# Moving ScalarE's guard work and the turning of K and B inside the steps of a fused recurrence and feed-forward kernel

## The chip, the cores and the metric

The kernel runs on one core of a Trainium2 chip. The metric is the device time of one execution in microseconds (us), the median of the runs shown. A core has five engines that run in parallel, each working off its own instructions in order: TensorE (PE in the profile; PEld is its loading of weights), VectorE (DVE), ScalarE (ACT), GpSimd (POOL) and SyncE (SP), which here only issues DMAs. TensorE writes its results to PSUM, a small memory of eight banks per partition; an engine that reads a PSUM buffer out sets when that buffer can be written again.

## The reference

Inputs r, k, v, w, a, b have the shape (4 batches, 8 heads, 768 tokens, 40). For each batch and head a 40x40 state is carried over the tokens, and its output goes through a feed-forward layer with squared ReLU:

```python
for t in range(S):
    y[:, :, t] = np.einsum('bhd,bhde->bhe', rt, state)
    Sa = np.einsum('bhde,bhe->bhd', state, at)
    state_decay = state * wt[:, :, None, :] - np.einsum('bhd,bhe->bhde', Sa, bt)
    state = state_decay + np.einsum('bhd,bhe->bhde', vt, kt)
...
x = attn_out.transpose(0, 2, 1, 3).reshape(B * S, H * D)
h = np.maximum(x @ w_in, 0.0)
out = (h * h) @ w_out        # w_in is 320 x 2048, w_out is 2048 x 320
```

## The kernel before

The 768 tokens are cut into 6 chunks of 128, so that the recurrence becomes matrix products inside a chunk and one hand-over from chunk to chunk. A chunk's 32 batch-head pairs are worked off in 8 steps of four heads: 48 steps `st` in all. Two steps make one batch m of inputs (one chunk of one batch, all eight heads, 24 of them). A loop over `st` (L603 on) writes the instructions of every engine in the order in which they are to run; nothing reorders them later. So a call's place in the loop's body is its place in the queue of each engine that it uses.

The names that matter:

- `st_a_mm` (ca on PE) and `st_a_ev` (CN on DVE, two instructions of 128x512): the masked products of the next step.
- `st_p`, `st_m`, `st_corr`, `st_c1`, `st_sn`: the inverse inside a chunk as a series. P is a PSUM tile; ScalarE copies it to Mc, PE adds a correction with Mc ("corr1", L339), DVE takes the difference c, PE adds a correction with c ("corr2", L339 again), and ScalarE copies the negated result, Sn, into the tile EVX (L355). POOL then makes x and Cc, where Cc waits for Sn.
- `st_jk` (L364): a square of the matrix N (a part of CN) with a running sum, on ScalarE; `st_energy` (L374, tile jm): squares of Mc or Cc of four earlier steps with a running sum, on ScalarE, in odd steps only. Both feed a guard that is tested after the loop (`ep`, L667). Each is two instructions: the activation and a short read of its accumulator.
- `st_t` (tb on PE, TB on DVE): Sn and the state U are transposed into one PSUM tile tb, Sn first, and copied to TB. `st_ex_mm` of the next step needs TB.
- `st_ex_mm`, `st_ex_ev`, `st_z`, `st_kb`, `st_y`: the output and the state (ex and uy on PE; EVX, YS and UZ on DVE).
- `filler(st)` takes the next piece of the feed-forward work of an earlier chunk; each step has three. In odd steps of the steady part the first two pieces are the two halves of an output (op, 8 matmuls each) and the third is a part of the hidden layer (hp, 6 matmuls); in even steps all three are hp. The copy that ends a piece runs on ScalarE: hs (ReLU) for hp, and osb, followed by the output DMA on SP, for the second half of op. With `hold=True` that copy is not written at once, but by `release()`, which comes behind `st_sn`; without it, it is written at once. The square of hs, Gt, runs on POOL, but for every fourth piece on DVE, and that one is put off to `flush()`, behind `st_t`. In the steady part it is the piece of the odd steps.
- `prepare(st, lot)` calls the steps by which a batch is prepared. For batches from 5 on: A's cast (POOL), the logarithm lnW (ACT), cs (PE), its two exponentials and KBp = K and B by an exponential (`prep_decay`: ACT, then POOL, odd steps), GA turned and copied (`prep_ga_mm`, `prep_ga_ev`: tt on PE, GT on ACT), AT (DVE), K and B turned and copied (`prep_kb`: 8 transposes into tt, then KBT on ACT, 128x1024), and the casts of V and R and two copies of V into EVX (POOL). The last ones, `prep_kb` and `prep_cast_rv`, have the lot 4, behind `st_t` and `flush()`.

hp, op, cs and tt share one PSUM tag, "ff", of two buffers, which they take in turn: each piece waits until the last piece but one has been copied out. P and tb share another, "sp".

Of the kernel before, what the change touches and what calls it, by code (L numbers as in the profile page):

```python
# [18 lines left out]
def kernel(  # L19
# [23 lines left out]
    NB, NHH, T, D = r.shape  # L43
# [4 lines left out]
    NQ = NP // 2  # L48
    NS = NCH * NQ
# [110 lines left out]
    def half(s):  # L160
        return slice(64 * s, 64 * s + 64)
# [132 lines left out]
    def st_a_mm(st):  # L294
        c, o, j0, p2, EVX = where(st)
        ca = CNs[st, "ps"] = [ps.tile([128, 2, 2, L], FP32, name=f"ca{s}", tag=f"ca{s}")
                              for s in range(2)]
        for u in range(2):
            for i in range(2):
                for s in range(2):  # L300
                    nc.tensor.matmul(out=ca[s][:, i, u, :], lhsT=o.KBT[half(s), u, j0 + i, :],  # L301
                                     rhs=o.AT[half(s), j0 + i, :], start=(i == 0 and u == 0),
                                     stop=True, skip_group_check=True)
# [7 lines left out]
    def st_p(st):  # L311
        c, o, j0, p2, EVX = where(st)
        CN, UZ = CNs[st], UZs[c % 2]
        P = Ps[st] = ps.tile([128, 2, 2, 64], FP32, name="P", tag="sp")
        if c > 0:
            for i in range(2):
                nc.tensor.matmul(
                    out=P[:, i, :, 0:D], lhsT=o.AT[:, j0 + i, :],
                    rhs=UZ[:, p2.start + i, :].rearrange("p (s d) -> p s d", s=2)[:, :, 0:D],
                    start=(i == 0), stop=False, skip_group_check=True)  # L320
        for i in range(2):
            for s in range(2):
                nc.tensor.matmul(out=P[:, i, s, 0:D], lhsT=CN[:, i, s, 0, :],  # L323
                                 rhs=EVX[:, i, s, L:LV], start=(c == 0 and i == 0 and s == 0),
                                 stop=False, skip_group_check=True)
# [18 lines left out]
    def st_c1(st):  # L344
        c, q = divmod(st, NQ)
        c1 = c1s[st] = qdp.tile([128, 4, D], BF16, name="c1", tag="c1")
        nc.vector.tensor_tensor(out=c1[:],  # L347
                                in0=Ps[st][:].rearrange("p i s e -> p (i s) e")[:, :, 0:D],
                                in1=Mc[c][:, q], op=ALU.subtract)
# [12 lines left out]
    def st_jk(st, CN):  # L362
        jk = qdp.tile([128, 2, 2, L], BF16, name="jk", tag="jk", bufs=1)
        nc.scalar.activation(out=jk[:], in_=CN[:, :, :, 1, :], func=ACTF.Square,  # L364
                             accum_out=ACC[:, AN + st:AN + st + 1])

    def st_energy(su):
        if su < 0 or su % 2 == 0:
            return
        hc = su // (NQ // 2)  # L370
        c, q = divmod(hc * (NQ // 2), NQ)
        src, at = ((Mc, AM), (Cc, AC))[su % (NQ // 2) // 2]
        jm = qdp.tile([128, NQ // 2, 4, D], BF16, name="jm", tag="jm", bufs=1)
        nc.scalar.activation(out=jm[:], in_=src[c][:, q:q + NQ // 2], func=ACTF.Square,  # L374
                             accum_out=ACC[:, at + hc:at + hc + 1])

    def st_t(st, su):
        tb = ps.tile([128, 4, 128], BF16, name="tb", tag="sp")
        if st < NS:
            EVX = EVXs[st % NEV]  # L380
            for i in range(2):
                for s in range(2):
                    nc.tensor.transpose(out=tb[half(s), i, :], in_=EVX[:, i, s, L + LV:EV],  # L383
                                        identity=IDb[:])
        if 0 <= su < NS - NQ:
            c, q = divmod(su, NQ)
            for i in range(2):
                for s in range(2):
                    nc.tensor.transpose(out=tb[half(s), 2 + i, :], identity=IDb[:],  # L389
                                        in_=UZs[(c + 1) % 2][:, 2 * q + i, half(s)])  # L390
        lo, hi = 0 if st < NS else 2, 4 if 0 <= su < NS - NQ else 2
        if lo < hi:
            TB = qdp.tile([128, 4, 128], BF16, name="TB", tag="TB", bufs=NQ + 2)
            nc.vector.tensor_copy(out=TB[:, lo:hi], in_=tb[:, lo:hi])  # L394
            SnTs[st] = TBs[su] = TB
# [3 lines left out]
    def st_ex_mm(st):  # L399
        c, o, j0, p2, EVX = where(st)  # L400
        SnT = SnTs.pop(st)
        ex = exs[st] = [ps.tile([128, 2, 2, L], FP32, name=f"ex{s}", tag=f"ex{s}")
                        for s in range(2)]
        for u in range(2):
            for i in range(2):
                for s in range(2):
                    lhsT = SnT[half(s), i, :] if u else o.RVT[half(s), 1, j0 + i, 0:L]
                    nc.tensor.matmul(out=ex[s][:, i, u, :], lhsT=lhsT,  # L408
                                     rhs=o.RVT[half(s), 0, j0 + i, 0:L],
                                     start=(i == 0 and u == 0), stop=True, skip_group_check=True)  # L410

    def st_ex_ev(st, s):
        EVX = EVXs[st % NEV]
        nc.vector.tensor_tensor(  # L414
            out=EVX[:, :, s, 0:2 * LV].rearrange("p i (u x) -> p i u x", u=2)[:, :, :, 0:L],
            in0=exs[st][s][:], in1=MEX[:].rearrange("p (i u) x -> p i u x", u=2), op=ALU.mult)
# [133 lines left out]
    def filler(st, hold=False):  # L550
        if fill and fill[0][0] <= st:
            fill.pop(0)[1](hold)
# [14 lines left out]
    for m in range(1, NBC):  # L567
        if m == 1:
            plan = ((-2, 1, prep_kb), (-2, 1, prep_ga), (-1, 4, prep_rv))
        elif m <= AHEAD:  # L570
            plan = ((-4, 5, prep_ln), (-4, 5, prep_decay), (-4, 5, prep_cast), (-3, 4, prep_kb),
                    (-3, 4, prep_ga), (-2, 4, prep_rv))
        else:
            plan = ((-4, "P" if m > AHEAD + 2 else 5, prep_new), (-4, 5, prep_ln),
                    (-3, "P", prep_decay), (-3, "C", prep_ga_mm), (-3, "C", prep_ga_ev),
                    (-3, "A", prep_at), (-3, 4, prep_kb), (-3, 4, prep_cast_rv),
                    (-2, "P", prep_v))
            plan += ((-2, 5, prep_turn),) if m >= 2 * NB else ((-1, 1, prep_rv),)
        if m >= AHEAD:
            plan += ((-9 if m == AHEAD else -7, 5, load),)  # L580
        for ds_, lot, f in plan:
            when.setdefault((2 * m + ds_, lot), []).append((f, m))

    def prepare(st, lot):
        for f, m in when.pop((st, lot), []):
            f(m)
# [15 lines left out]
    Ns = {}  # L602
    for st in range(NS + 2):  # L603
        late = st == 1
        if st + 1 < NS and not late:
            st_a_mm(st + 1)
        if 1 <= st <= NS:
            st_ex_mm(st - 1)
        if st < NS:
            st_p(st)  # L610
            st_m(st)
        if 1 <= st <= NS:
            st_jk(st - 1, Ns.pop(st - 1))
        if st >= 2:
            st_y(st - 2)
        if 1 <= st <= NS:
            st_ex_ev(st - 1, 0)
        prepare(st, "P")
        filler(st)
        if 1 <= st <= NS:  # L620
            st_z(st - 1)
        if st < NS:
            st_corr(st, Mc[st // NQ][:, st % NQ], False)
            st_c1(st)
        prepare(st, "C")
        if 1 <= st <= NS:
            st_ex_ev(st - 1, 1)
        prepare(st, "A")
        if st + 1 < NS and not late:
            st_a_ev(st + 1)  # L630
        filler(st, True)
        if st == 0:
            warm(8)
        prepare(st, 1)
        if st < NS:
            st_corr(st, c1s[st], True)
            Ns[st] = st_sn(st)
        release()
        if late:
            st_a_mm(st + 1)  # L640
        filler(st)
        st_t(st, st - 2)
        if late:
            st_a_ev(st + 1)
        flush()
        prepare(st, 4)
        if st >= NS - 4:
            filler(st)
        st_energy(st - NQ // 2)
        if 1 <= st <= NS:  # L650
            st_kb(st - 1)
        if 1 <= st <= NG:
            load_win(st - 1)
        if st == 4:
            load_wout()
        if st >= 2 and (st - 2) % (NQ // 2) == NQ // 2 - 1:
            h = (st - 2) // (NQ // 2)
            gather(*divmod(h, 2), [nc.sync] if st < NS + 1 else [nc.sync, nc.gpsimd, nc.sync])
            feed(st + 2, h)
        prepare(st, 5)  # L660
# [137 lines left out]
```

## Time and profile before

| what | us |
|---|---|
| runs shown: 311.32, 308.99, 312.38; median | 311.32 |
| the profiled execution's own time | 310.16 |
| its span, from the first to the last instruction | 308.4 |

Parts 1 and 2 of the profile's page: busy time of each engine, its share of the span and its instructions, and the span in 40 slices, where a digit is the busy share in tenths.

```profile
PE 281.4 (91%) x3746; PEld 212.1 (69%) x3746; DVE 221.1 (72%) x503; ACT 203.6 (66%) x529; POOL 210.2 (68%) x390
...
PE   7766887799999999999999999999999999898892
...
DVE  7456676798879878887978798788879776841140
ACT  3454336487688778777877887787787776645260
POOL 8575745388876887797779779777977886625200
PEclk9985755799999999999999999999999999979799
```

The first quarter, up to about 75 us, is the start: inputs and weights are loaded, and TensorE's granted clock is at half for a part of it. From about 78 to 260 us the steps run steadily. Behind it comes a tail, in which the rest of the feed-forward work drains.

Part 4, the chain of work that ended last, by engine, and two groups of part 5 (line, engine, operation, out<-in, count, busy time and mean of one in ns, idle time of the engine before them and what ended it):

```profile
PE 64%; ACT 21%; DVE 5%; issue 4%; POOL 3%; DVEq 0%; ACTq 0%; POOLq 0%
...
L364 ACT ACTIVATE jk<-CN 128x512 bf16<-128x512 bf16 x48 | 30.0, 624 | 0.0
```
```profile
L374 ACT ACTIVATE jm<-Mc 128x640 bf16<-128x640 bf16 x12 | 8.7, 728 | 0.0
L374 ACT ACTIVATE jm<-Cc 128x640 bf16<-128x640 bf16 x12 | 8.7, 728 | 0.0
```

A chain's shares say which engine's work each moment of the span is put down to, followed back from the last instruction. Durations of neighbours on one engine overlap by about 0.1 us, so sums of them are a little more than the time that they take.

### The profile page before, as it was taken

What the parts mean: (1) busy time and instruction counts of PE and PEld (TensorE: products, weight loads), DVE (VectorE), ACT (ScalarE), POOL (GpSimd) and SP (SyncE); (2) the same over time, 40 slices, a digit from 0 to 9 for tenths busy, and PEclk for the clock granted to TensorE, in tenths of its full rate; (3) what the DMA queues carried; (4) which work ended last, traced back from release to release, by engine and by line L of the source; (5) the groups of instructions that cost most, each with busy time, mean ns of one, the idle gap of its engine ahead of it and who ended that gap; (6) DMA issues with size and microseconds to landing.
All of it is one profiled execution on the core that took longest, in us unless ns stands there. A gap on an engine that the chain in (4) does not pass through costs nothing.

```text
span 308.4 us, 9648 instructions
## 1 busy us (share of the span) xinstructions
PE 281.4 (91%) x3746; PEld 212.1 (69%) x3746; DVE 221.1 (72%) x503; ACT 203.6 (66%) x529; POOL 210.2 (68%) x390
## 2 busy tenths in 40 slices
PE   7766887799999999999999999999999999898892
PEld 5545555567777777777777777777777777665581
DVE  7456676798879878887978798788879776841140
ACT  3454336487688778777877887787787776645260
POOL 8575745388876887797779779777977886625200
PEclk9985755799999999999999999999999999979799
DMA  7989789785572993977948929949958522000001
GB/s 131 186 153 170 131 125 178 123 141 95 102 130 51 175 154 70 184 141 122 180 83 144 176 62 188 159 89 177 133 98 168 114 41 57 27 23 26 24 23 52
DMA packets 175349, 35.54 MB, mean 115 GB/s; under 512 B 169840, under 2 KB 174976, under 8 KB 175296
## 3 DMA queue, kind: packets, MB, share of 16 engines
q1 hardware_dynamic: 172656, 32.22, 59.4%
q0 software_dynamic: 2640, 2.63, 5.4%
q8 instruction: 31, 0.51, 0.8%
q14 instruction: 22, 0.18, 0.2%
HBM read 28.84 MB, written 3.93 MB: 106 GB/s over the span
## 4 chain that ended last, share of the span: by engine, by line
PE 64%; ACT 21%; DVE 5%; issue 4%; POOL 3%; DVEq 0%; ACTq 0%; POOLq 0%
PE hp L499 12%; PE tt L222 10%; ACT KBT L236 7%; PE cs L203 5%; ACT jm L374 5%; ACT hs L510 4%; PE tb L383 4%; PE ca L301 3%; PE uy L433 3%; PE P L339 2%; PE ex L408 2%; ACT jk L364 2%; ACT Mc L332 2%; PE tb L389 1%; DVE CN L309 1%
## 5 line engine op out<-in xcount | busy, mean ns | idle before, releaser
L511 POOL TENSOR_TENSOR Gt<-hs 128x512 bf16<-128x512 bf16 x66 | 67.9, 1044 | 39.9 <-ACT hs L510 39.9
L499 PE MATMUL hp<-YS,WIN 120*128 120x256 bf16 (+1 forms) x576 | 77.4, 271 | 1.3
L414 DVE TENSOR_TENSOR EVX<-ex,MEX 128x512 bf16<-128x512 f32 x96 | 65.8, 686 | 5.6 <-PE ex L408 3.7
L510 ACT ACTIVATE hs<-hp 128x512 bf16<-128x512 f32 x96 | 56.9, 595 | 7.9 <-PE hp L499 5.3
L309 DVE TENSOR_TENSOR CN<-ca,MCN 128x512 bf16<-128x512 f32 x96 | 61.3, 680 | 0.8 <-PE ca L301 0.8
L499 PEld LDWEIGHTS <-WIN 120*128 120x128 bf16 (+1 forms) x576 | 50.9, 96 | 8.8 <-issue 2.9
L532 PEld LDWEIGHTS <-Gt 128*128 128x128 bf16 x384 | 37.5, 101 | 18.2 <-issue 3.5
L347 DVE TENSOR_TENSOR c<-P,Mc 128x160 bf16<-128x160 f32 x48 | 15.5, 324 | 35.6 <-PE P L339 34.6
L236 ACT ACTIVATE KBT<-tt 128x1024 bf16<-128x1024 bf16 x24 | 24.6, 1024 | 13.5 <-PE tt L222 13.4
L214 POOL TENSOR_TENSOR KBp<-NK,GI 128x320 bf16<-128x320 f32 x24 | 21.0, 874 | 15.8 <-ACT GI L206 11.7
L358 POOL TENSOR_TENSOR x<-Mc,c 128x160 f32<-128x160 bf16 x48 | 23.4, 488 | 11.3 <-DVE c L347 11.3
L339 PEld LDWEIGHTS <-CN 128*128 128x128 bf16 x384 | 22.6, 98 | 12.4 <-issue 8.5
L364 ACT ACTIVATE jk<-CN 128x512 bf16<-128x512 bf16 x48 | 30.0, 624 | 0.0
L359 POOL TENSOR_TENSOR Cc<-x,EVX 128x160 bf16<-128x160 f32 x48 | 23.5, 489 | 6.9 <-ACT EVX L355 3.6
L332 ACT ACTIVATE Mc<-P 128x160 bf16<-128x160 f32 x48 | 14.4, 300 | 20.1 <-PE P L323 20.1
L355 ACT ACTIVATE EVX<-P 128x160 bf16<-128x160 f32 x48 | 14.6, 304 | 18.7 <-PE P L339 18.5
L433 PE MATMUL uy<-EVX,KBp 128*64 128x168 bf16 x384 | 24.4, 253 | 0.0
L443 DVE TENSOR_TENSOR YS<-uy,GT 128x256 bf16<-128x256 f32 x48 | 20.0, 418 | 4.9 <-PE uy L433 4.7
L511 DVE TENSOR_TENSOR Gt<-hs 128x512 bf16<-128x512 bf16 x30 | 16.5, 549 | 9.0 <-ACT hs L510 8.8
L301 PE MATMUL ca<-AT,KBT 64*128 64x128 bf16 x384 | 22.2, 232 | 0.2
L203 PE MATMUL cs<-lnW,UTI 128*128 128x320 f32 x48 | 21.4, 532 | 0.4 <-POOL RV L148 0.4
L394 DVE COPY TB<-tb 128x512 bf16<-128x512 bf16 (+1 forms) x48 | 18.9, 394 | 2.1 <-PE tb L383 2.0
(137 smaller groups left out, 572.8 us busy)
## 6 DMA issues: line engine op xcount, KB each, us to landing
NW<-in_w_dram SPq DMA_DIRECT2D x24, 160.0 KB, 3.6
NK<-in_k_dram SPq DMA_DIRECT2D x24, 160.0 KB, 3.5
NB<-in_b_dram SPq DMA_DIRECT2D x24, 160.0 KB
NA<-in_a_dram SPq DMA_DIRECT2D x24, 160.0 KB, 3.7
NV<-in_v_dram SPq DMA_DIRECT2D x24, 160.0 KB, 3.7
NR<-in_r_dram SPq DMA_DIRECT2D x24, 160.0 KB, 3.8
out_dram<-osb SPq DMA_DIRECT2D x24, 160.0 KB, 2.2
WOUT<-in_moe_w_out_dram POOLq DMA_DIRECT2D x1, 1280.0 KB, 13.1
```

The costliest lines, as they stand in the source:

```text
L203: nc.tensor.matmul(out=cs[:].rearrange("p h e -> p (h e)"), lhsT=UTI[:], rhs=o.lnW[:], start=True, stop=True)
L222: nc.tensor.transpose(out=t_[:, u, j, :], identity=IDb[:], in_=pad[:, u, 2 * j:2 * j + 2, :].rearrange("p a b -> p (a b)"))
L236: nc.scalar.activation(out=o.KBT[:], in_=t2[:], func=ACTF.Copy)
L301: nc.tensor.matmul(out=ca[s][:, i, u, :], lhsT=o.KBT[half(s), u, j0 + i, :], rhs=o.AT[half(s), j0 + i, :], start=(i == 0 and u == 0), stop ...
L309: nc.vector.tensor_tensor(out=CN[:, :, s], in0=ca[s][:], in1=MCN[:], op=ALU.mult)
L364: nc.scalar.activation(out=jk[:], in_=CN[:, :, :, 1, :], func=ACTF.Square, accum_out=ACC[:, AN + st:AN + st + 1])
L414: nc.vector.tensor_tensor(out=EVX[:, :, s, 0:2 * LV].rearrange("p i (u x) -> p i u x", u=2)[:, :, :, 0:L], in0=exs[st][s][:], in1=MEX[:].r ...
L433: nc.tensor.matmul(out=uy[half(s), i, :], lhsT=o.KB[:, u, 2 * (j0 + i) + s, :], rhs=EVX[:, i, s, LV * u:LV * u + LV], start=(c == 0 and i ...
L499: nc.tensor.matmul(out=hp[:, u, :].rearrange("p (a b) -> p a b", a=HB), lhsT=WIN[g][0:ROWS[g], j * 128:(j + 1) * 128], rhs=by_pair(c, hf)[ ...
L510: nc.scalar.activation(out=hs[:], in_=flat, func=ACTF.Relu)
L511: later.append(lambda: eng.tensor_tensor(out=out_, in0=hs[:], in1=hs[:], op=ALU.mult))
L532: nc.tensor.matmul(out=op_[:], lhsT=Gts[c, hf][:, j, b_, :], rhs=WOUT[:, j, :], start=(j == 0), stop=(j == NJ - 1))
```

## The change

Five edits, all of them to the order of instructions; none is added, dropped or resized.

1. `prep_kb` (K and B turned, and their copy KBT) gets a lot of its own, "T", in front of `st_t`, for batches from 5 on. It falls in odd steps.
2. In even steps `st_jk` is written behind the first filler instead of ahead of `st_y`; in odd steps it stays.
3. `st_energy` moves from near the end of the step to behind `st_c1`, ahead of lot "C" (where GA is turned and GT copied).
4. The second filler is held back in even steps only; in odd steps its copy is written at once, ahead of `st_sn`.
5. The call of lot "T" stands between the third filler and `st_t`.

```diff
-                    (-3, "A", prep_at), (-3, 4, prep_kb), (-3, 4, prep_cast_rv),
+                    (-3, "A", prep_at), (-3, "T", prep_kb), (-3, 4, prep_cast_rv),
...
-        if 1 <= st <= NS:
+        if 1 <= st <= NS and st % 2:
             st_jk(st - 1, Ns.pop(st - 1))
         if st >= 2:
             st_y(st - 2)
...
         prepare(st, "P")
         filler(st)
+        if 1 <= st <= NS and st % 2 == 0:
+            st_jk(st - 1, Ns.pop(st - 1))
         if 1 <= st <= NS:
             st_z(st - 1)
         if st < NS:
             st_corr(st, Mc[st // NQ][:, st % NQ], False)
             st_c1(st)
+        st_energy(st - NQ // 2)
         prepare(st, "C")
...
-        filler(st, True)
+        filler(st, st % 2 == 0)
...
         filler(st)
+        prepare(st, "T")
         st_t(st, st - 2)
...
-        st_energy(st - NQ // 2)
         if 1 <= st <= NS:
             st_kb(st - 1)
```

## The prediction

> **What bounds the kernel now.** The sums of each engine over windows come first: from 100 to 260 us TensorE is busy some 19.85 us of every 20, VectorE 16.4, ScalarE 15.6, POOL 15.8, at a granted clock of 1.00, which I leave as it is. TensorE's figure can't be taken as it stands, because neighbouring matmuls overlap. So I read the chain of waits over one odd step and the even step after it (a "pair", from one cs matmul to the next: 14 pairs from 100.55 to 249.39 us, 10.63 us each).
>
> ```profile
> 147.49 0.23 PE tb L383 x4
> 147.72 0.11 PE tb L389 x4
> 147.83 0.57 PE tt L222 x8
> 148.40 0.02 issue
> 148.42 1.02 ACT KBT L236
> 149.44 0.72 ACT jm L374 x2
> 150.16 0.18 ACT Mc L332
> 150.34 0.42 issue
> 150.76 0.20 ACT jk L364
> 150.96 0.50 ACT hs L510
> 151.46 0.04 issue
> 151.50 0.82 PE hp L499 x6
> ```
>
> The chain leaves TensorE once per pair. The turned K and B (tt) are the last thing of the odd step, so their copy KBT is late on ScalarE; jm runs behind it, then the even step's Mc, jk and hs, and filler 3's matmul waits at 151.50 for the PSUM buffer that hs reads. Next, ScalarE's and VectorE's timelines of the same stretch (start, duration, engine, line; idle before, and what ended it), with one Gt row of VectorE and its POOL neighbour from a pair that began at 68.02.
>
> ```profile
> 145.68 0.60 ACT L269 ACTIVATE GT<-tt 128x512 bf16<-128x512 bf16 x1 [0.66 <-PE tt L222]
> 146.86 0.30 ACT L355 ACTIVATE EVX<-P 128x160 bf16<-128x160 f32 x1 [0.58 <-PE P L339]
> 147.06 0.43 ACT L538 ACTIVATE osb<-op__3152 128x320 f32<-128x320 f32 x1
> ```
> ```profile
> 147.87 0.42 DVE L394 COPY TB<-tb 128x512 bf16<-128x512 bf16 x1
> 148.21 0.64 DVE L511 TENSOR_TENSOR Gt<-hs 128x512 bf16<-128x512 bf16 x1
> ...
> 150.80 0.33 DVE L347 TENSOR_TENSOR c<-P,Mc 128x160 bf16<-128x160 f32 x1 [0.42 <-PE P L339]
> ...
> 152.83 0.41 DVE L394 COPY TB<-tb 128x512 bf16<-128x512 bf16 x1
> ```
> ```profile
> 148.13 0.46 POOL L256 CAST RVp<-NR 128x320 bf16<-128x320 f32 x1
> ```
> ```profile
> 73.70 0.42 DVE L511 TENSOR_TENSOR Gt<-hs 128x512 bf16<-128x512 bf16 x1
> ```
> ```profile
> 73.53 0.77 POOL L196 COPY EVX<-RVp 128x160 bf16<-128x160 bf16 x2
> ```
>
> VectorE idles only 0.42 us between the two TB rows. That is the second bound: the odd step's TB starts a queue TB, Gt, YS, UZ, EVX, c, EVX, CN, CN, TB, and the next odd step's ex waits for the last TB.
>
> **The change part by part**, in us from the cs at 143.07.
>
> *Squares jm into odd steps' hole.* ScalarE finishes GI at 145.02 and waits 0.66 for GT at 145.68 (2.61). jm takes 0.63 to its accumulator read and 0.09 to the next: 0.72, but it starts 0.10 after GI's read starts (144.81), so at 144.91 and out of the way at 145.63. Cost 0. If tt came earlier, GT would slip by up to 0.72, onto AT and CN. Removed behind KBT: 0.72.
>
> *Filler 2 not held in odd steps.* There it is always the second half of an output, so its copy osb moves ahead of Sn; its output DMA enters SP's queue some 0.3 earlier, ahead of the same loads, transposes and gathers as now. op ends at 3.65, osb runs from 3.67, Sn from 4.00 (osb's 0.43 less the 0.10 overlap of neighbours) instead of 3.79. Behind Sn wait Cc on POOL and the turning of Sn, which now comes at 4.81. Cost 0 here; it frees the PSUM buffer that tt needs at 4.26. If that cover fails: 0.21.
>
> *K and B turned ahead of Sn and U.* Nothing is added: 8 transposes change places with 8. Today hp takes 0.76 to the next group, tb 0.13 and 0.21, tt 0.55: 1.65 from 146.66 to 148.31. These are steps from a group's first matmul to the next group's. A group takes 0.09 to 0.11 more where the tile shape changes behind it (tt on GA, with no change behind it, 0.44; tb on UZ, 0.11 in the even step). The new order has one change instead of three: hp 0.67, tt 0.55, tb 0.13, 0.11, sum 1.46, so TensorE gains 0.19. KBp is ready at 3.70, before 4.26. The price: tb stands behind tt, so TB starts at 3.59+0.67+0.55+0.13+0.32 = 5.26 instead of 4.80 (0.32 from the transposes of U to TB, 147.55 to 147.87), and everything behind TB on VectorE with it, +0.46. In front of tt on TensorE nothing moves; behind it wait Sn's and U's transposes, uy, ca and ex.
>
> *The even step's Mc and jk.* TensorE leaves U at 5.05; by the same rows uy takes 0.40, ca 0.25, ex 0.11 and 0.21, P 0.08 and 0.10, hp 0.67, uy from U 0.14, corr1 0.10, hp 0.67, corr2 0.10. On ScalarE hs of filler 3 now runs at 4.51, KBT at 5.01 to 6.03, and nothing behind it. The P matmuls run at 6.10, so Mc starts at 6.39 (0.29 behind them, as in odd steps), against 6.99; corr1 runs at 7.01 against 7.33. hs of filler 1 starts at 7.04, jk follows to 8.15, and Sn, ready at 8.04, starts at 8.16, before TensorE wants it at 8.63. With Mc this early jk in its old place would let hs end at 7.79, still ahead of 7.88: that edit is worth about 0. Filler 3's matmul starts at 7.88, against 8.43. If jk's cover goes, Sn is late by jk's own 0.61 at most.
>
> *What is late next.* VectorE. The pair at 68.02 shows this queue without idle time: TB 73.37, c 75.50, TB 77.52, next cs 78.40, that is 2.13, 2.02 and 0.88; its first TB came at 5.35 and it took 10.38. The changed pair is 5.26+2.13+2.02+0.88 = 10.29, 0.34 less. c at 5.26+2.13 = 7.39 is just in time for corr2 at 7.78 (0.37 from c to corr2 today). TensorE alone, with 0.75, 0.13, 0.11, 0.39, 0.26 and 0.12 from filler 3's hp to the second half of ex and 0.40 on to cs, would be at cs at 10.04; it waits 0.25 for TB.
>
> The unknown is Gt, 0.42 there but 0.64 here. At 148.21 it starts 0.08 into POOL's cast of R and ends 0.26 after it; at 73.70 it starts after that cast, beside the EVX copies. In the changed pair Gt starts at 5.60 and the cast ends at about 5.74 (Cc 0.45 after Sn's start, as in the one pair where it waited for Sn; 0.43 and 0.40 on to the cast, whose own is 0.46), so Gt would end near 6.02: I take 0.42. Bounds: 0.42, its time with nothing beside it too (in the tail), and to the end of the EVX copies plus 0.26, at about 6.7.
>
> The Trainium skill (GPSIMD Engine Reference, Specifications) says that GpSimd shares its SBUF interfaces with VectorE and that instructions with two SBUF inputs contend. Gt is one, and the copies beside it at 73.70 didn't slow it: taken to the letter, for every POOL access, the rule would end Gt at about 6.7 and give the slower rival below; the row gives my sum.
>
> *Where it counts.* Pairs that begin from 78.40 to 249.39 us: 17, and 17 x 0.34 = 5.8. In those at 58.37 and 68.02 POOL delivers KBp late (70.89+0.87) or VectorE is already the bound: 0. The pairs at 78.40 and 89.47 take 11.07, as VectorE copies RV (0.60) ahead of TB and TensorE turns RV (0.45) ahead of corr2; with both, TB comes at 5.71 instead of 5.37 and the pair takes 5.71+5.03 = 10.74, a gain of 0.33, so they count like the rest. Steps up to 6 have no fillers and the old plan: 0. In the tail the jm at 284.79 leaves the run of two jm before ep (0.72), and the 0.24 wait of op at 278.52 goes: 1.0. The sum is 6.8.
>
> The profiled run took 310.2 (its span of 308.4 and 1.8 around it): 310.2 - 6.8 = 303.4. The median of the runs shown, 311.3, is 1.2 above that run, which would give 304.5; I take the middle, 304, and add 0.6 to each rival in the same way.
>
> **The rivals.** *TensorE becomes the bound* (VectorE catches up): 17 x 0.59 + 1.0 = 11.0, so 300. For it: its row of 19.85 in 20. Against: the queue above has nothing left to drop. 0.08.
>
> *Gt stays at 0.64* (the cast moves along with it): YS then starts 0.62 after Gt as today, c at 7.67, TB at 9.69, the next cs at 10.57, 0.06 less than now: 17 x 0.06 + 1.0 = 2.0, so 309; no change to speak of. For it: 14 regular pairs show 0.64 to 0.65. 0.16.
>
> *Slower: Gt falls under POOL's copies of V.* They run from 5.7 to 6.45 and hold Gt until 6.7; YS then starts at 6.64, c at 8.09, 0.37 after today's 7.72, TB too, and a pair takes 11.0: 17 x 0.37 - 1.0 = +5.3, so 316. It decides once Gt takes more than about 0.77. For it: Gt already stretches beside the cast. Against: 73.70, and 0.53 at 84.09, where Gt ends 0.27 after the cast with the copies beginning. 0.13.
>
> *jm doesn't fit the hole*: the margin is 0.05, GT slips by a tenth, AT and CN too, and TB at 5.26 still has 0.46 spare: inside the forecast.
>
> **How the numbers follow.** Forecast 0.63, rivals 0.08, 0.16, 0.13. The range 299 to 309.5 takes in all but the slower rival, and with it the spread of the runs around each case. A measurement of this kernel can tell about 1%, 3.1 us. Faster: 0.63+0.08+a quarter of 0.16 = 0.75; the same 0.12, the rest of it; slower 0.13.
>
> **What would show it.** Pairs of 10.3 us; jm between GI and GT; Mc of even steps waiting for TensorE, not behind jm; no hp waiting for hs; TB of odd steps at 5.26 from cs, and VectorE without idle time before c in even steps; TensorE waiting some 0.25 for TB before ex. Wrong if Gt takes 0.64 or more, if tt waits for osb or KBp, or if Sn holds up tb.

## The result: 2.8% faster, and the chain has moved from ScalarE to VectorE

The changed kernel takes 302.23 us (median of 6 runs, 300.36 to 303.62) against 310.74 for the kernel before (6 runs beside it, 308.99 to 312.38): a ratio of 0.9722, with a 95% interval of 0.9675 to 0.9769. The forecast was 304 with a range of 299 to 309.5. The profiled run took 300.36 us, with a span of 298.5; it is the fastest of the six.

Parts 1 and 4 of the changed kernel's page, busy time by engine and the chain's shares by engine and line:

```profile
PE 271.2 (91%) x3746; PEld 208.7 (70%) x3746; DVE 216.1 (72%) x503; ACT 200.3 (67%) x529; POOL 210.4 (71%) x390
...
PE 57%; DVE 28%; ACT 8%; issue 3%; POOL 2%; DVEq 0%; ACTq 0%; POOLq 0%
```

ScalarE's share of the chain fell from 21% to 8%, VectorE's rose from 5% to 28%. The busy shares show nothing of this: no engine's share moved by more than three points. A pair (one odd and one even step, from cs to cs) now takes 10.285 us, as a mean over 14 pairs, against 10.631. This is the chain of waits over such a pair of the changed kernel, from the odd step's tt on; left out are UZ and steps of a few hundredths (start, duration, what; the pair's cs starts at 140.57 on TensorE's own timeline; in this view a step begins where the one before it ends, so it can be shorter than the instruction):

```profile
144.98 0.45 PE tt L222 x8
145.43 0.23 PE tb L383 x4
145.66 0.13 PE tb L389 x4
...
145.81 0.42 DVE TB L394
146.24 0.34 DVE Gt L511
146.58 0.33 DVE YS L443
...
147.35 0.54 DVE EVX L414
...
147.96 0.31 DVE c L347
148.27 0.60 DVE EVX L414
148.87 1.21 DVE CN L309 x2
...
150.12 0.38 PE ca L301 x7
```

Where the chain of before went tt, KBT, jm, Mc, jk, hs, it now goes tt, tb, and then through VectorE's whole queue from TB to the second CN, 4.3 us without a hole to speak of. ScalarE's timeline of the same stretch shows why it has left the chain (last column: idle time before, and what ended it):

```profile
142.39 0.74 ACT L374 ACTIVATE jm<-Cc 128x640 bf16<-128x640 bf16 x1
...
143.17 0.60 ACT L269 ACTIVATE GT<-tt 128x512 bf16<-128x512 bf16 x1
144.25 0.44 ACT L538 ACTIVATE osb<-op__3152 128x320 f32<-128x320 f32 x1 [0.49 <-PE op__3152 L532]
144.59 0.30 ACT L355 ACTIVATE EVX<-P 128x160 bf16<-128x160 f32 x1
145.08 0.60 ACT L510 ACTIVATE hs<-hp 128x512 bf16<-128x512 f32 x1 [0.19 <-PE hp L499]
145.57 1.02 ACT L236 ACTIVATE KBT<-tt 128x1024 bf16<-128x1024 bf16 x1
146.93 0.30 ACT L332 ACTIVATE Mc<-P 128x160 bf16<-128x160 f32 x1 [0.34 <-PE P L323]
```

jm fills the hole ahead of GT and GT is not late for it (2.60 from cs, as before). KBT starts 0.35 earlier, and the even step's Mc now waits for TensorE, not for ScalarE.

The last wait of the chain stands one instruction earlier than I had said. TensorE does not first wait at ex for TB, but at ca, which writes the PSUM that CN is still reading. TensorE's weight loads and matmuls at that place of the changed kernel:

```profile
150.12 0.20 PEld L301 LDWEIGHTS <-KBT 64*128 64x128 bf16 x6 [0.21 <-issue]
```
```profile
149.81 0.68 PE L301 MATMUL ca<-AT,KBT 64*128 64x128 bf16 x8
```

The eight matmuls of ca, 0.40 elsewhere, are spread over 0.68, and six of their weights wait 0.21.

### The profile page after: what moved, and what is told of

The parts are those of the page before. It is cut to its first block, busy times and chain, and to the rows that moved or that the text cites. A ratio compares the mean times of both kernels' runs of the same rounds, so it can differ in the third digit from the quotient of the medians.

```text
span 298.5 us, 9666 instructions
## 1 busy us (share of the span) xinstructions
PE 271.2 (91%) x3746; PEld 208.7 (70%) x3746; DVE 216.1 (72%) x503; ACT 200.3 (67%) x529; POOL 210.4 (71%) x390
## 4 chain that ended last, share of the span: by engine, by line
PE 57%; DVE 28%; ACT 8%; issue 3%; POOL 2%; DVEq 0%; ACTq 0%; POOLq 0%
PE tt L222 9%; DVE CN L309 8%; PE hp L499 8%; DVE EVX L414 7%; PE cs L203 5%; PE ca L301 4%; DVE c L347 3%; PE ex L408 3%; DVE UZ L448 2%; PE tb L383 2%; DVE TB L394 2%; PE P L339 2%; DVE Gt L511 2%; DVE YS L443 2%; PE uy L433 2%
## 5 line engine op out<-in xcount | busy, mean ns | idle before, releaser
L510 ACT ACTIVATE hs<-hp 128x512 bf16<-128x512 f32 x96 | 55.3, 599 | 16.6 <-PE hp L499 16.0
L499 PEld LDWEIGHTS <-WIN 120*128 120x128 bf16 (+1 forms) x576 | 49.6, 96 | 6.7 <-issue 0.8
L532 PEld LDWEIGHTS <-Gt 128*128 128x128 bf16 x384 | 36.5, 98 | 16.3 <-issue 3.1
L359 POOL TENSOR_TENSOR Cc<-x,EVX 128x160 bf16<-128x160 f32 x48 | 23.4, 488 | 10.6 <-ACT EVX L355 8.4
L339 PEld LDWEIGHTS <-CN 128*128 128x128 bf16 x384 | 22.1, 97 | 10.4 <-issue 8.2
L301 PE MATMUL ca<-AT,KBT 64*128 64x128 bf16 x384 | 24.7, 232 | 1.5 <-DVE CN L309 0.2
L301 PEld LDWEIGHTS <-KBT 64*128 64x128 bf16 x384 | 13.2, 99 | 12.0 <-issue 6.6
L448 DVE TENSOR_TENSOR UZ<-uy,GT 64x80 bf16<-64x80 f32 x80 | 18.7, 233 | 0.5
```

The source lines that it names most:

```text
L339: nc.tensor.matmul(out=P[:, i, s, 0:D], lhsT=CN[:, i, s, 1, :], rhs=X[:, 2 * i + s], start=False, stop=last, skip_group_check=True)
L499: nc.tensor.matmul(out=hp[:, u, :].rearrange("p (a b) -> p a b", a=HB), lhsT=WIN[g][0:ROWS[g], j * 128:(j + 1) * 128], rhs=by_pair(c, hf)[ ...
L510: nc.scalar.activation(out=hs[:], in_=flat, func=ACTF.Relu)
L532: nc.tensor.matmul(out=op_[:], lhsT=Gts[c, hf][:, j, b_, :], rhs=WOUT[:, j, :], start=(j == 0), stop=(j == NJ - 1))
```

## The experiments

The time of a whole kernel is a blunt tool here: runs of one kernel spread by 3 us and more, and the part before the steady pairs as well as the tail differ from run to run. Each kernel has one profile; in it the first 13 of the 14 steady pairs agree to 0.03 us or better, and three kernels for which the same pair was expected (changed, turn without squares, jk back) agree to 0.003 us in the mean. So each kernel is judged by its mean over 14 pairs. The last of the 14 is shorter in some of them, because VectorE's short products UZ fall away in it; where that matters, the mean of the other 13 is given beside it.

| kernel | pair, us | expected | whole kernel, us |
|---|---|---|---|
| before | 10.631 | | 310.74 |
| changed | 10.285 | 10.29 | 302.23 |
| squares only | 10.500 | 10.48 | 303.66 (4 runs) |
| turn without squares | 10.286 | 10.29 to 10.32 | 305.29 (4 runs) |
| filler 2 held | 10.599 | 10.49 | 307.75 (1 run) |
| squares without turn | 10.530 | 10.47 | 305.85 (4 runs) |
| POOL shifted | 10.423 | 10.49 | 305.56 (1 run) |
| more on VectorE, changed | 10.626 | 10.58 | 309.00 (1 run) |
| more on VectorE, before | 10.631 | 10.63 | 311.05 (1 run) |
| cs early | 10.087 | 10.11 | 297.82 (4 runs) |
| jk back | 10.288 | 10.29 | 302.12 (1 run) |
| cs early, before | 10.659 | 10.7 | 311.81 (1 run) |

### Which of the edits carries the gain

Four kernels take the change apart. The first has the squares alone, on top of the kernel before:

```diff
             st_c1(st)
+        st_energy(st - NQ // 2)
         prepare(st, "C")
...
-        st_energy(st - NQ // 2)
         if 1 <= st <= NS:
             st_kb(st - 1)
```

> The kernel before with one edit of the change alone: the squares jm stand behind c instead of at the end of odd steps. My theory (three bounds close together: ScalarE's run before Mc, TensorE's way to corr1, VectorE's queue from TB to TB): Mc of even steps no longer waits for jm but for the P matmuls at 6.29, so it starts at 6.58 instead of 6.99; corr1 runs at 7.19, c at 7.58 instead of 7.72, TB at 9.6, and a pair takes 10.48 us instead of 10.63 (0.15 of the 0.34 that the change gains). The whole kernel: 0.15 x 17 and about 1 in the tail, some 3.5 us. Rival 1 (ScalarE's run is the only bound and the squares are the whole of the gain): 10.29. Rival 2 (the turning is the whole of it): 10.63.

Measured 10.500, my theory's 10.48 and neither rival's. The ratio of the whole kernel to the one before is 0.9828 (0.9762 to 0.9894), that is some 5.3 us (3.3 to 7.4) where 3.5 were expected. Its chain of waits shows the next bound, at Mc and c of the even step:

```profile
146.47 0.11 PE P L323 x4
...
146.60 0.30 ACT Mc L332
146.90 0.38 ACT jk L364
...
147.61 0.33 DVE c L347
```

Mc follows the P matmuls at once. The chain's step through jk is how the view names the 0.7 us up to c, as jk was ScalarE's last work in it; what c needs is corr1, and the row for c in VectorE's timeline of the kernel before names it: L339.

The second is the change without the squares, and with jk in its old place (changed kernel as the base):

```diff
-        st_energy(st - NQ // 2)
         prepare(st, "C")
...
+        st_energy(st - NQ // 2)
         if 1 <= st <= NS:
             st_kb(st - 1)
```

> The changed kernel with the squares jm back at the end of odd steps and jk back ahead of the fillers in even steps; the turning of K and B ahead of Sn and filler 2 not held stay. My theory: KBT now ends so early that jm behind it lets Mc start at 6.65, just in time for corr1 at 6.99; jk ahead of hs costs 0.24 at filler 3's hp, which TensorE has to spare before it waits for TB. A pair takes 10.29 to 10.32 us, as in the whole change; only the tail lacks about 1 us, so the whole kernel is some 1 us slower than the changed one. Rival 1 (the squares are the gain): 10.5 or more.

Measured 10.286: the steady pair of the full change, without its edits 2 and 3. The squares add nothing once K and B are turned early, since KBT then ends early enough to leave room for jm. From the last cs to the guard's test (`ep`) this kernel takes 35.58 us, the changed one 34.85: 0.73, which the squares cost where they stand late again; the granted clock is 1.00 in that stretch of both. The ratio to the kernel before is 0.9858 (0.9778 to 0.9938).

The third holds filler 2 back again:

```diff
-        filler(st, st % 2 == 0)
+        filler(st, True)
```

> The changed kernel with filler 2 held back in odd steps again, so that osb comes behind Sn. My theory: osb runs at 3.99 to 4.42 instead of 3.69 to 4.13, tt must wait for its PSUM buffer until 4.46 instead of running at 4.25, TB comes 0.2 later, and a pair takes 10.49 us: this edit carries 0.20 of the 0.34. Rival (it is only a detail, tt does not wait for osb): 10.29.

Measured 10.599, so the expected step is there and a second one with it. tt starts 0.21 later (4.46 from cs), TB too (5.46), as expected: tt does wait for osb. The other 0.10 is Gt, which took 0.53 to 0.54 instead of 0.42. These are VectorE's and POOL's timelines of one such pair:

```profile
117.28 0.54 DVE L511 TENSOR_TENSOR Gt<-hs 128x512 bf16<-128x512 bf16 x1
```
```profile
116.95 0.58 POOL L196 COPY EVX<-RVp 128x160 bf16<-128x160 bf16 x2
117.48 0.65 POOL L256 CAST GAp<-NA 128x320 bf16<-128x320 f32 x1
```

Gt began while the second copy of V was under way, ended 0.27 after it (117.81 against 117.54, by the trace's unrounded times), and POOL's next cast took 0.65 instead of its usual 0.46. Without this one edit nine tenths of the gain in a pair are lost: 0.31 of 0.35. The prediction's price for a tt that waits for osb was 0.21; the part of Gt was not in it.

The fourth leaves the turning out and keeps the rest:

```diff
-                    (-3, "A", prep_at), (-3, "T", prep_kb), (-3, 4, prep_cast_rv),
+                    (-3, "A", prep_at), (-3, 4, prep_kb), (-3, 4, prep_cast_rv),
```

> The changed kernel with the turning of K and B back behind Sn's and U's transposes; squares, jk and filler 2 stay as changed. My theory: TB of odd steps is early again (4.80), but TensorE gets to corr1 only at 7.19, so c starts at 7.58 instead of 7.39 and a pair takes 10.47 us. Rival 1 (the squares are the gain, the turning only moves a wait from ScalarE to VectorE): 10.29 or less. Rival 2 (without the turning nothing is gained): 10.63.

Measured 10.530, between the rivals and 0.06 over my number. corr1 ran at 7.23 from cs, where I had 7.19; the third hp takes 0.78 to tb here, 0.03 more than before; Sn, which the next group turns, now stands behind osb. The ratio to the kernel before is 0.9899 (0.9829 to 0.9969).

A fifth put jk back alone:

```diff
-        if 1 <= st <= NS and st % 2:
+        if 1 <= st <= NS:
             st_jk(st - 1, Ns.pop(st - 1))
...
-        if 1 <= st <= NS and st % 2 == 0:
-            st_jk(st - 1, Ns.pop(st - 1))
```

> The changed kernel with jk of even steps back ahead of the fillers. My theory, as predicted: this edit is worth nothing. With Mc at 6.36, jk runs to 7.18 and hs of filler 1 from there, its buffer is free at 7.8, and filler 3's hp wants it at 7.86: a pair takes 10.29 us. Rival (jk ahead of hs is a part of the chain, as it was in the kernel before): 10.5.

Measured 10.288: worth nothing, as predicted. hs of filler 1 ran at 7.17 instead of 7.09, still in time.

### Is VectorE's queue the bound?

The same idle memset was put on VectorE, behind the odd step's Gt, in both kernels:

```diff
         flush()
+        if st % 2 and 5 <= st < NS:
+            nc.vector.memset(dud[:], 0.0)
         prepare(st, 4)
```

> The changed kernel with one memset of 128x400 f32 more on VectorE (about 0.36 us, 0.30 of its queue) behind Gt in odd steps. Nothing waits for it. My theory: VectorE's queue between the two TB has no idle time left, so a pair takes 10.58 us, the 10.285 of the changed kernel and the whole 0.30. Rival (TensorE is the bound now): 10.29 to 10.35.

> The same memset in the same place of the kernel before. My theory: there VectorE idles for 0.42 us ahead of c, as c waits for corr1, so the 0.30 go into that hole and a pair stays at 10.63 us. Rival (VectorE's queue was the bound before, too): 10.93.

Measured 10.626 and 10.631. In the kernel before, 0.39 us more of VectorE's work cost nothing at all; in the changed one they cost 0.34. Over the 13 regular pairs it is 0.37 (10.654 against 10.287), as much as c moves (7.76 from cs instead of 7.39): all that the memset takes from the queue. VectorE's rows from TB to the next c, first the changed kernel with the memset, then the kernel before with it:

```profile
161.75 0.42 DVE L396 COPY TB<-tb 128x512 bf16<-128x512 bf16 x1 [0.40 <-PE tb L391]
162.09 0.42 DVE L513 TENSOR_TENSOR Gt<-hs 128x512 bf16<-128x512 bf16 x1
162.54 0.39 DVE L653 MEMSET dud<- 128x400 f32 x1
...
164.25 0.31 DVE L347 TENSOR_TENSOR c<-P,Mc 128x160 bf16<-128x160 f32 x1
```
```profile
148.74 0.42 DVE L396 COPY TB<-tb 128x512 bf16<-128x512 bf16 x1
149.08 0.64 DVE L513 TENSOR_TENSOR Gt<-hs 128x512 bf16<-128x512 bf16 x1
149.75 0.39 DVE L649 MEMSET dud<- 128x400 f32 x1
...
151.66 0.33 DVE L347 TENSOR_TENSOR c<-P,Mc 128x160 bf16<-128x160 f32 x1
```

From TB to c the second takes 2.92, exactly the time without the memset (it was 7.72 - 4.80): the memset went into the hole. The first takes 2.50 instead of the 2.14 of the changed kernel.

### Does POOL's work beside Gt cost time?

```diff
     def prep_cast_rv(m):
+        nc.gpsimd.memset(dum[:], 0.0)
         cast(m, "V")
```

> The changed kernel with one memset of 128x128 f32 more on POOL (about 0.2 us) ahead of the casts of V and R in odd steps. No instruction that is on the path waits for these casts. My theory, from Gt's rows in six kernels (0.65 where POOL's cast began just before it, 0.42 where nothing or only the end of one did, 0.53 in the held variant, where the second copy of V was under way): Gt does not start before the POOL instruction that is under way has ended, and takes some 0.27 from there, at least 0.42 in all. The cast of R then runs at 5.49 to 5.94 with Gt at 5.59, Gt ends at 6.21 instead of 6.01, takes 0.62, and everything behind it on VectorE moves by 0.2: a pair takes 10.49 us instead of 10.29. Rival (POOL's work beside Gt costs nothing that counts, VectorE has spare time): 10.29.

Measured 10.423. POOL's queue moved by 0.15, not 0.2, so R's cast ended at 5.89 from cs, and Gt, at 5.59 as before, took 0.57 instead of 0.42: it ended 0.27 after the cast. The rows of one pair, whose cs is at 142.59:

```profile
148.18 0.57 DVE L514 TENSOR_TENSOR Gt<-hs 128x512 bf16<-128x512 bf16 x1
```
```profile
148.02 0.46 POOL L256 CAST RVp<-NR 128x320 bf16<-128x320 f32 x1
```

The pair grew by 0.14 (by 0.15 over the 13 regular pairs), so a POOL instruction that nothing on the path waits for costs what it adds to Gt. My number was too high because I took the memset's duration for its share of the queue.

### A version that beats both

If VectorE's queue is the bound and TensorE waits 0.25 for it at ca and ex, work of TensorE's that needs neither can stand there. cs is such work, if the logarithm that it reads is ready:

```diff
-            plan = ((-4, "P" if m > AHEAD + 2 else 5, prep_new), (-4, 5, prep_ln),
-                    (-3, "P", prep_decay), (-3, "C", prep_ga_mm), (-3, "C", prep_ga_ev),
+            plan = ((-4, "P" if m > AHEAD + 2 else 5, prep_new), (-4, "L" if m > AHEAD + 2 else 5, prep_ln),
+                    (-3, "Q" if m > AHEAD + 2 else "P", prep_decay), (-3, "C", prep_ga_mm), (-3, "C", prep_ga_ev),
...
         late = st == 1
+        prepare(st, "Q")
...
         prepare(st, "P")
+        prepare(st, "L")
         filler(st)
```

> The changed kernel, and in odd steps cs with its two exponentials and KBp (the whole of that preparation step) goes to the head of the step, ahead of ca, with the logarithm lnW behind the even step's Mc instead of at its end. In the changed kernel TensorE's ca at 9.24 waits for VectorE's last CN (it reads the PSUM that ca writes) until 9.5, and ex for TB until 9.88, while cs behind them needs neither. My theory: cs fills that wait. TensorE then runs cs at 9.24 to 9.9, ca at 9.96, ex with TB at 10.34 and op at 10.73 instead of 10.905; one more change of the tile shape costs 0.1 of it. A pair takes 10.11 us, and the whole kernel is about 3 us faster than the changed one, near 299.5. Rival (something else, such as lnW, hs or POOL, holds cs there): 10.29 or more.

Measured 10.087, and 297.82 us for the whole (4 runs, 296.02 to 298.52), a ratio to the kernel before of 0.9591 (0.9535 to 0.9646), whose interval lies below that of the change. The chain of waits over the place in question has no other engine in it any more:

```profile
138.90 0.29 PE uy L433 x8
139.19 0.74 PE cs L203 x2
139.93 0.33 PE ca L301 x8
140.25 0.22 PE ex L408 x8
140.48 0.18 PE P L317 x2
```

cs takes 0.74 to the next group instead of 0.63, which is the change of the tile shape. The control is the same move in the kernel before, with the logarithm behind the even step's Sn:

```diff
+        prepare(st, "Q")
...
+        prepare(st, "L")
         release()
```

> The kernel before with the same move of cs, its exponentials and KBp to the head of odd steps; the logarithm lnW stands behind Sn of the even step, where ScalarE has it ready in time and nothing on the path waits for it. My theory: the wait that an early cs fills in the changed kernel (ca for CN, ex for TB) is not there in the kernel before, as VectorE idles ahead of c; so nothing is gained, the additional change of the tile shape costs 0.1, and a pair takes 10.7 us. Rival (the wait was there before, too, and the change only left it): 10.4 or less.

Measured 10.659, 0.03 more than without it. So the wait that cs fills was not there before; the change made it, and it is part of what the change cost.

## Why the prediction was right

*What bounds the kernel.* Right. The second bound that I had named behind ScalarE's run, VectorE's queue from TB to TB, is the bound now: the two memsets show it from both sides.

*Squares.* Cost 0 as predicted: jm at 1.82 from cs, GT still at 2.60. Their worth in the pair was not stated apart; alone they gain 0.13, on top of the turning nothing.

*Filler 2.* Sn starts at 4.02 (said: 4.00) and holds up nothing; tt starts at 4.25 (said: 4.26). That the edit frees the buffer for tt was right, and it turned out to decide: without it 0.31 of the 0.35 are gone, where the prediction had put 0.21.

*The turning.* TB at 5.25 (said: 5.26); TensorE spends 1.45 from hp to uy (said: 1.46) instead of 1.65.

*Even step.* Mc at 6.36 (6.39), corr1 at 6.98 (7.01), c at 7.39 (7.39), corr2 at 7.76 (7.78), TB at 9.41 (9.41), the pair 10.285 (10.29). jk's move is worth 0, as said.

*What is late next.* VectorE, right; the wait stands at ca for CN as much as at ex for TB, which I had missed. It cost the sum nothing, as both end at the same time.

*Gt.* The term that I was least sure of came out at 0.42, but for a reason that I had read too narrowly. I took the row at 73.70 to say that POOL's copies of V don't slow Gt. They do, as the held kernel shows. At 73.70 the copy under way ended early enough, and in the changed kernel R's cast ends 0.15 after Gt has begun (146.31 against 146.16), which leaves Gt its 0.42:

```profile
146.16 0.42 DVE L511 TENSOR_TENSOR Gt<-hs 128x512 bf16<-128x512 bf16 x1
```
```profile
145.85 0.46 POOL L256 CAST RVp<-NR 128x320 bf16<-128x320 f32 x1
```

The number was right by a narrow margin, then: had R's cast come 0.15 later, as with POOL shifted, a pair would have lost 0.15. Here the Trainium skill (GPSIMD Engine Reference, Specifications), which lets a VectorE instruction with two SBUF inputs contend with GpSimd, was nearer to the truth than my row. The slower rival, Gt held until the last of POOL's copies had ended, did not come: Gt waits for one instruction, not for the queue.

*The size.* 6.8 us were worked out for the profiled run; the two profiled runs differ by 9.8, and the medians by 8.5 (from the interval 7.2 to 10.1). The steady part is as predicted: from the cs at 78.40 to the one at 249.39 the kernel before takes 170.99 us, the changed one 165.58 for the same pairs, 5.4 less for 16 of the 17 pairs.

The tail, put at 1.0, differs by 3.9 between the two profiled runs, and most of that is TensorE's clock. In the profile before, the granted clock is 0.50 from 270 to 272 us, ahead of the guard's test, and again from 288 to 290 us, right behind it; in the profile after it is 1.00 from 250 to 296 us. The same matmuls take longer there. These are two groups of the kernel before, then the same two of the changed one:

```profile
270.14 2.30 PE L532 MATMUL op__6194<-WOUT,Gt 128*128 128x320 bf16 x8
286.82 4.02 PE L532 MATMUL op__6400<-WOUT,Gt 128*128 128x320 bf16 x16
```
```profile
263.95 1.25 PE L532 MATMUL op__6194<-WOUT,Gt 128*128 128x320 bf16 x8
278.56 2.35 PE L532 MATMUL op__6400<-WOUT,Gt 128*128 128x320 bf16 x16
```

Behind the test, where the instructions are the same, this makes 1.67: up to ScalarE's last instruction that part takes 16.6 us in the profile before and in five of the experiments, each with the clock near 0.5 right behind the test, and 14.95 in the profile after and the other five. Ahead of the test it makes 1.55: the kernel `turn without squares` has a clock of 1.00 there, and from 15.5 to 20.5 us behind the last cs its TensorE runs the same groups as the kernel before at the same offsets to 0.02 us; then the clock falls in the profile before, and it comes to the test 1.55 later. What is left for the change is 0.73, the squares. The 0.34 that was counted for the 17th pair is not in it: TensorE is 0.40 ahead at 11.65 us behind the last cs, but only 0.11 at 15.5.

So of the 9.8 us between the profiled runs the change has 5.4 + 0.7 = 6.1, 0.7 less than the sum, with the tail's terms too high; the clock has 3.2. The changed profile is also ahead by 0.6 at the first cs of a pair that was to change (57.75 against 58.37), but that cs comes anywhere from 54.84 to 59.76 in the twelve profiles. That the total landed so near the forecast is therefore in part luck. How much of the 8.5 between the medians is the clock stays open, since only one execution of each kernel has a profile. The stretch at half clock ahead of the test is there in all four kernels that are built on the one before, and in none of the eight built on the changed one; whether the order of instructions has a part in that, no run shows.

## What to carry to other kernels

When a wait is taken off one engine, add up the next engine's queue between the same two events before hoping for the whole of it: here ScalarE's run, TensorE's way to corr1 and VectorE's queue lay within 0.4 us of each other in a pair of 10.6, so no single edit could gain more than the distance to the next: the squares alone gained 0.13, while the turning with filler 2, which brings both Mc and corr1 forward, gained all of it. The edit that looks like a detail can carry the rest: an early transposition is worth nothing while the PSUM buffer that it needs is copied out late. And once the bound has moved, ask which of the waiting engine's own work needs nothing of the new bound; moving that one piece gained more than half as much again.

## What the runs showed of the hardware

VectorE's product of two SBUF tiles (Gt) and POOL's casts and copies shut each other out, one instruction at a time. If a POOL instruction is under way when Gt starts, Gt ends some 0.27 us after it, as it does in each of the 14 steady pairs of all twelve profiles (0.27 to 0.28; Gt itself takes 0.65 beside the cast of R in the kernel before, 0.57 with POOL shifted, 0.54 in the held kernel); a POOL instruction that wants to start while Gt runs stretches instead (0.65 for a cast of 0.46). If the neighbour ends within the first 0.15 us, nothing is seen. Moving a cast by 0.15 us changed the kernel's pair by 0.14.

TensorE takes 0.09 to 0.11 us more between groups whose tile shapes differ, at the full granted clock: turning K and B ahead of Sn and U saves two such changes, and an early cs pays one (0.74 instead of 0.63). The Trainium skill (TensorEngine Tiling (Array Packing), Key Properties) says that a change of the tiling mode drains TensorE; it gives no time, and this is what it cost here.

In the tail TensorE's granted clock fell to half in some executions and not in others. Between the kernel before and `turn without squares` the groups ahead of it are the same and stand at the same offsets to 0.02 us; one has 0.50 there, the other 1.00. Sixteen matmuls take 4.02 us instead of 2.35 where it falls right behind the test. What sets it off is not shown.
